# An attention and two mixtures of experts on one core: scores of packed rows in 64x32 tiles, w_in kept as two parts, raw weights in w_out's room

## The chip, the cores and the metric

The kernel runs on one NeuronCore of a Trainium2 chip. The core has a matrix engine (TensorE, PE in the profile, with PEld for its weight loads), VectorE (DVE), ScalarE (ACT), GpSimd (POOL) and SyncE (SP), which only issues transfers here. Each engine works through its own list in order and waits on semaphores. Work memory is SBUF (128 partitions); TensorE writes to PSUM, from where the other engines copy. The metric is the device time of one launch in microseconds; lower is better.

## The reference

```python
def sm_attn(qq, kk, vv):                     # q, k, v: (8, 8, 576, 64); p: (8, 8, 32, 64)
    s = scale * np.matmul(qq, kk.transpose(0, 1, 3, 2))
    s = s - np.max(s, axis=-1, keepdims=True)
    a = np.exp(s)
    a = a / (np.sum(a, axis=-1, keepdims=True) + 1e-09)
    return np.matmul(a, vv)
p_packed = sm_attn(p, k, v)                  # 32 packed rows per head
x = heads side by side of sm_attn(q, p_packed, p_packed)     # (4608, 512)
g = np.maximum(x @ w_in, 0.0) ** 2           # w_in (512, 2048), float64
x = (g @ w_out).astype(np.float32)           # w_out (2048, 512), float64
logits = x @ w_gate + log1p(exp(x @ w_noise)) * noise        # 8 experts
two best experts per token, softmax of their logits as weights
out[token] += weight * (np.maximum(x @ w1[e], 0.0) @ w2[e])  # 512 -> 1024 -> 512
```

The weights w_in and w_out are float64; everything else is float32.

## The kernel before

The work falls into stages. **Packed rows.** For each of 8 batches and two groups of four heads (`part1`, units "A"), 32 packed rows per head attend to 576 keys: scores (`u_s`), maximum, exponent, transposition, product with the values, and a transposition into `pk`, the packed rows with the head dimension on partitions. **Decode.** w_in and w_out come as 64-bit words in 32 chunks of 128 rows by 512 (`decode`, units "d", loads "r"). From the two 32-bit words of a number, ScalarE (`o0`) and VectorE (`o2` to `o5`) make a float32 high part `dec_a` and a bfloat16 rest `dec_b`. For w_in, TensorE adds the two (`o6`) and ScalarE copies the float32 sum into `win` (`o8`). For w_out, a rounded high part and a low part go into `wo`. Raw words lie in four buffers `st`. **Fold.** For each batch and quarter of w_in (`prepare`, units "P"), eight tiles of 64x32 on TensorE multiply packed rows with w_in, so that the second attention and the first layer become one product (`heads`); the result goes as high and low part into `ring`. **Second attention** (`part2`, units "Q"): for each of 16 blocks of 288 tokens, scores of queries with packed rows, softmax, and the attention weights turned into `xT`. **First mixture** (`moe_step`, units "M"): for each block, 16 steps of a first layer (6 matmuls), square, split into `gh` and `gl`, and a second layer (12 matmuls) into four PSUM banks `acc`. At a block's end ScalarE and VectorE copy `acc` to `x2T` (`moe_x2`), VectorE turns it into `x2s` (`x2_turn`, units "X"), and SyncE stores it; logits and routing follow ("R", "U"). **Experts**: tokens are gathered by GpSimd's indirect transfers, and for each of 8 experts in three tiles of rows (512, 384, and 256 with 64 more for four experts) `e_l1` and `e_l2` run two layers; `e_out` weights the rows, and GpSimd adds them to the output.

All precise products are sums of three float32r matmuls over high and low parts (`TERMS`). The order of the first 15 blocks is made by a planner (`schedule`): each unit has an engine, a cost in ns, predecessors and a priority (its longest path to the end and a lead by kind, `AHEAD`); while TensorE would be idle for over 500 ns in the first 45 us of the plan, groups of four matmuls of ones (L1119) are put into its list. Block 15 and the experts are in an order that is written out by hand, in steps that lag two behind each other.

Of the kernel before, what the change touches and what calls it, by code (L numbers as in the profile page):

```python
# [45 lines left out]
STB = 4  # L46
NFF = FF // P
LAG = 2
TB = 3
# [8 lines left out]
AHEAD = {"r": 74, "d": 54.7, "D": 17.3, "a": 113.6, "A": 57.6, "q": 30.5, "Q": 4.5, "p": 73.7, "P": 5.9, "R": 96.4, "M": 1.2, "s": 26.5, "S": 31.5}  # L58
DUE = 11
# [27 lines left out]
def program(ctx, tc, qT, kT, v, v5, pT, w_in, w_out, wg, wn, noise, w1, w2, out):  # L87
# [24 lines left out]
    wo = cst.tile([P, NFF, 2, DM], FR, name="wo")  # L112
# [57 lines left out]
    win = wi.tile([P, 4, FF], F, name="win")  # L170
    att, c_att = open_pool("att", "left")
# [29 lines left out]
    def decode(n):  # L201
# [1126 lines left out]
```

## Time and profile before

| | us |
|---|---|
| median of 3 runs | 1711.03 |
| lowest, highest | 1709.98, 1712.17 |
| the profiled execution | 1707.94 |
| its span, first to last instruction | 1706.1 |
| TensorE busy | 1653.8 |
| VectorE busy | 858.8 |
| ScalarE busy | 638.3 |
| GpSimd busy | 539.4 |

The profiled execution is one run; 1.84 us of its time lie outside the span. A busy time is the union of an engine's instructions; for TensorE the ends are modelled and neighbours overlap, so the price of a piece of its work is better read from the starts.

### The profile page before, as it was taken

The numbers are of one execution on the slowest core, as the hardware profiler recorded it, in microseconds if no ns is written. First come the engines' busy times: TensorE is split into PE (matmuls) and PEld (weight loads), VectorE is DVE, ScalarE is ACT, GpSimd is POOL, SyncE is SP. The second block draws the span as 40 slices with busy tenths as digits, with TensorE's granted clock in tenths as the row PEclk, the third lists the DMA queues.
The fourth block names the chain that finished last, engine by engine and source line by source line (L and its number), as shares of the span: only waits on it lengthen the run. The fifth ranks groups of instructions, "written<-read, shape, count | busy, mean of one in ns | idle before, by whom it ended". The sixth has DMA issues, their size and how long they took to land. (4 is left out here: it accounts for less than half of the span.)

```text
span 1706.1 us, 28402 instructions
## 1 busy us (share of the span) xinstructions
PE 1653.8 (97%) x11054; PEld 1428.1 (84%) x11054; DVE 858.8 (50%) x2008; ACT 638.3 (37%) x1372; POOL 539.4 (32%) x500
## 2 busy tenths in 40 slices
PE   9999999999999999997997999999999999999996
PEld 7678989889898998996786788888888878888785
DVE  6973757565666847474543543333343343434321
ACT  4875444453534445345422222222222232223211
POOL 0000110203020212115326446445364462635611
PEclk9999999999999999999998999999999999999998
DMA  8743142313223202013334434334353443425312
GB/s 258 216 124 87 29 125 54 92 48 91 75 69 97 75 19 59 15 28 91 69 60 102 94 77 102 75 82 98 64 110 71 83 106 63 110 67 103 59 25 32
DMA packets 125343, 140.79 MB, mean 83 GB/s; under 512 B 33055, under 2 KB 87327, under 8 KB 125207
## 3 DMA queue, kind: packets, MB, share of 16 engines
q1 hardware_dynamic: 101975, 100.05, 21.0%
q0 software_dynamic: 23232, 38.90, 13.3%
q8 instruction: 88, 1.44, 0.4%
q14 instruction: 48, 0.39, 0.1%
HBM read 99.71 MB, written 39.19 MB: 81 GB/s over the span
## 5 line engine op out<-in xcount | busy, mean ns | idle before, releaser
L688 PE MATMUL acc<-gh,wo 128*128 128x288 f32 x2048 | 426.5, 301 | 6.6 <-issue 6.6
L688 PEld LDWEIGHTS acc<-gh,wo 128*128 128x128 f32 x2048 | 328.6, 189 | 36.8 <-issue 28.8
L876 DVE SCALAR_TENSOR_TENSOR hl<-ph,hh 128x512 fp32r<-128x512 f32 (+3 forms) x184 | 105.6, 574 | 450.0 <-ACT hh L875 354.4
L843 POOL DMA_INDIRECT xg<-x2d,gi x296 | 295.1, 997 | 90.3 <-issue 87.8
L688 PE MATMUL acc<-gl,wo 128*128 128x288 f32 x1024 | 303.0, 296 | 6.2 <-DVE gl L679 3.1
L875 ACT ACTIVATE hh<-ph 128x512 fp32r<-128x512 f32 (+3 forms) x184 | 92.9, 505 | 504.1 <-PE ph L869 367.2
L652 PE MATMUL ph<-xT,ring 128*128 128x288 f32 x1536 | 245.3, 300 | 4.6 <-issue 3.2
L620 POOL DMA_INDIRECT lst<-ent,pi x96 | 92.6, 965 | 475.3 <-DVE pi L599 238.8
L652 PEld LDWEIGHTS ph<-xT,ring 128*128 128x128 f32 x1536 | 214.8, 189 | 27.2 <-issue 14.6
L869 PE MATMUL ph<-ring,wo 128*128 128x512 f32 (+3 forms) x1152 | 225.8, 344 | 10.4 <-issue 9.3
L898 POOL DMA_INDIRECT out<-y,ls x76 | 125.4, 1650 | 348.9 <-DVE y L895 174.4
L869 PE MATMUL ph<-ring,wb 128*128 128x512 f32 (+3 forms) x1152 | 224.7, 343 | 3.6 <-ACT ring L105 1.9
L869 PEld LDWEIGHTS ph<-ring,wo 128*128 128x128 f32 x1152 | 196.4, 190 | 35.0 <-issue 11.0
L869 PEld LDWEIGHTS ph<-ring,wb 128*128 128x128 f32 x1152 | 194.3, 188 | 29.0 <-ACT ring L105 2.8
L688 PEld LDWEIGHTS acc<-gl,wo 128*128 128x128 f32 x1024 | 193.5, 189 | 9.1 <-DVE gl L679 5.1
L659 ACT ACTIVATE g<-ph 128x288 f32<-128x288 f32 x256 | 104.4, 408 | 242.7 <-PE ph L652 228.7
L886 PE MATMUL acc<-wo,hh 128*128 128x512 f32 (+1 forms) x608 | 193.3, 399 | 0.0
L886 PE MATMUL acc<-wb,hh 128*128 128x512 f32 (+1 forms) x576 | 179.6, 393 | 0.3 <-issue 0.3
L674 DVE TENSOR_TENSOR g<-g 128x288 f32<-128x288 f32 x208 | 101.8, 490 | 116.8 <-ACT gh L665 113.4
L679 DVE TENSOR_TENSOR gl<-g,gh 128x288 fp32r<-128x288 f32 x256 | 117.4, 459 | 54.6 <-ACT gh L105 38.5
L886 PEld LDWEIGHTS acc<-wo,hh 128*128 128x128 f32 (+1 forms) x608 | 111.7, 187 | 23.2 <-issue 0.7
L886 PEld LDWEIGHTS acc<-wb,hh 128*128 128x128 f32 (+1 forms) x576 | 104.8, 185 | 21.4 <-issue 0.8
(202 smaller groups left out, 1763.0 us busy)
## 6 DMA issues: line engine op xcount, KB each, us to landing
wst<-w SPq DMA_DIRECT2D x128, 256.0 KB
out<-zero SPq DMA_DIRECT2D x37, 256.0 KB
q<-qT SPq DMA_DIRECT2D x16, 576.0 KB
x2d<-x2s SPq DMA_DIRECT2D x64, 144.0 KB
kq<-kT SPq DMA_DIRECT2D x15, 576.0 KB
st<-w_in SPq DMA_DIRECT2D x16, 512.0 KB
st<-w_out SPq DMA_DIRECT2D x16, 512.0 KB
vq<-v SPq DMA_DIRECT2D x15, 512.0 KB
```

The source lines that it names most:

```text
L620: nc.gpsimd.indirect_dma_start(out=lst, out_offset=bass.IndirectOffsetOnAxis(ap=st["pi"][:, r, k:k + 1], axis=0), in_=st["ent"][:, r, k], ...
L652: nc.tensor.matmul(ph, w[:, a, d], xT[j, b][:, d], start=n == 0, stop=n == 5)
L659: nc.scalar.activation(g, ph, AF.Relu)
L674: nc.vector.tensor_mul(g, g, g)
L679: nc.vector.tensor_sub(gl, g, gh.bitcast(F))
L688: nc.tensor.matmul(acc[j][d], wo[:, f, b, d * P:(d + 1) * P], g[a], start=f == 0 and n == 0, stop=f == NFF - 1 and n == 2)
L843: nc.gpsimd.indirect_dma_start(out=g[:, x], out_offset=None, in_=src, in_offset=bass.IndirectOffsetOnAxis(ap=idx, axis=0))
L869: nc.tensor.matmul(ph, wblock(e, f, a)[:, c], xt[t][b][:, c, :n], start=i == 0, stop=i == 11)
L875: nc.scalar.activation(hh, ph, AF.Relu)
L876: nc.vector.scalar_tensor_tensor(hl, ph, 0.0, hh.bitcast(F), op0=OP.max, op1=OP.subtract)
L886: nc.tensor.matmul(acc["e", t, r], h[a][:, o:o + n], wblock(e, 8 + f, b).rearrange("p c f -> p (c f)"), start=first and i == 0, stop=last ...
L898: nc.gpsimd.indirect_dma_start(out=out, out_offset=bass.IndirectOffsetOnAxis(ap=sl[:, 0:1], axis=0), in_=y, in_offset=None, compute_op=OP.add)
```

## The change

The scores of packed rows were four matmuls over 128 rows of the array, with packed rows padded with zeros and two columns of tiles. Now they are eight matmuls in tiles of 64x32, one for each of four heads and half of the keys; the host lays out keys and packed rows accordingly. w_in is no longer summed: its high part lies in `win` (float32), its rest in `wint` (bfloat16), and the fold multiplies packed rows with the one and a bfloat16 copy of them, `pk16`, with the other. Raw words are loaded into the room that w_out's finished chunks will take (`wo` is now 16 tiles), which leaves more loads in flight. The second attention's two buffers become one tile of two halves, and `x2s` of the first 14 blocks shares it. In the experts, the extra 64 rows keep high and low part side by side in `pair`, so that one matmul with 128 columns of weights does for two, and `e_out` adds two halves. The planner's leads, costs and due times change.

```diff
-AHEAD = {"r": 74, "d": 54.7, "D": 17.3, "a": 113.6, "A": 57.6, "q": 30.5, "Q": 4.5, "p": 73.7, "P": 5.9, "R": 96.4, "M": 1.2, "s": 26.5, "S": 31.5}
-DUE = 11
+AHEAD = {'r': 77.6, 'o': 80.4, 'd': 83.1, 'D': 20.1, 'a': 85.1, 'A': 60.8, 'q': 35.6, 'Q': 1.1, 'p': 60.4, 'P': 5.9, 'R': 96.4, 'M': 0.9, 's': 34.6, 'S': 32.0}
+DUE = 0
...
-    wo = cst.tile([P, NFF, 2, DM], FR, name="wo")
+    wo = [None] * NFF
+
+    def wo_room(i, shape, dt):
+        return cst.tile(shape, dt, name=f"wo{i}", bufs=1)
...
     win = wi.tile([P, 4, FF], F, name="win")
+    wint = wi.tile([P, 4, FF], BF, name="wint")
...
-        raw[n] = stg.tile([P, 512, 2], I32, name="st", bufs=STB)
+        raw[n] = wo_room(i if kind else 8 + i % 8, [P, 2 * DM], I32)
...
         def o2():
-            st["a"] = stg.tile([P, 512], I32, name="dec_a", bufs=TB)
+            if kind:
+                st["a"] = four(stg.tile([P, 512], I32, name="dec_a", bufs=TB))
+            else:
+                st["a"] = win[:, :, P * i:P * i + P].bitcast(I32)
             nc.vector.tensor_scalar(st["a"], st["t"], 3, 0x7FFFFFFF, op0=OP.logical_shift_left, op1=OP.bitwise_and)
...
         def o5():
-            st["b"] = stg.tile([P, 512], BF, name="dec_b", bufs=2)
-            nc.vector.scalar_tensor_tensor(st["b"], raw[n][:, :, 0].bitcast(U32), 2.0 ** -52, st["t"].bitcast(F),
+            st["b"] = four(stg.tile([P, 512], BF, name="dec_b", bufs=2)) if kind else wint[:, :, P * i:P * i + P]
+            nc.vector.scalar_tensor_tensor(st["b"], words(n, 0).bitcast(U32), 2.0 ** -52, st["t"].bitcast(F),
                                            op0=OP.mult, op1=OP.mult)
...
         def o6():
             st["s"] = side("sum", [P, 512])
-            nc.tensor.matmul(st["s"], ident, st["a"].bitcast(F), start=True, stop=False)
-            if kind:
-                nc.tensor.matmul(st["s"], minus, wo[:, i, 0], start=False, stop=False)
-            nc.tensor.matmul(st["s"], ident16, st["b"], start=False, stop=True)
+            nc.tensor.matmul(st["s"], ident, st["a"].bitcast(F).rearrange("p c f -> p (c f)"), start=True, stop=False)
+            nc.tensor.matmul(st["s"], minus, wo[i][:, 0], start=False, stop=False)
+            nc.tensor.matmul(st["s"], ident16, st["b"].rearrange("p c f -> p (c f)"), start=False, stop=True)
...
         def o7():
-            act_copy(wo[:, i, 0], st["a"].bitcast(F))
+            wo[i] = wo_room(i, [P, 2, DM], FR)
+            act_copy(four(wo[i][:, 0]), st["a"].bitcast(F))
...
         def o8():
-            if kind:
-                act_copy(wo[:, i, 1], st["s"])
-            else:
-                act_copy(win[:, :, P * i:P * i + P], st["s"].rearrange("p (c f) -> p c f", c=4))
+            act_copy(wo[i][:, 1], st["s"])
 
         x = ("d", n)
-        unit(("r", n), "sp", load, [("d", n - STB, 5)], dma=524288)
+        if kind:
+            old = [("d", chunks.index((0, i)), 5)] if i >= 8 else []
+        else:
+            old = [("d", chunks.index((0, i - 8)), 5)] if i >= 8 else []
+        unit(("r", n), "sp", load, old, dma=524288)
...
-        unit(x + (2,), "dve", o2, [x + (0,), ("d", n - TB, 6)], 417)
+        unit(x + (2,), "dve", o2, [x + (0,)] + ([("d", chunks.index((1, i - TB)), 6)] if kind and i >= TB else []) +
+             (lent if not kind and i >= LENT_FROM else []), 417)
...
-        unit(x + (5,), "dve", o5, [x + (4,), ("d", n - 2, 6)], 680)
+        unit(x + (5,), "dve", o5, [x + (4,)] + ([("d", chunks.index((1, i - 2)), 6)] if kind and i >= 2 else []), 680)
         if kind:
-            unit(x + (7,), "act", o7, [x + (3,)], 620)
-        unit(x + (6,), "pe", o6, [x + (5,), x + (7,)] + (lent if not kind and i >= LENT_FROM else []), 1560 if kind else 1300,
-             psum=(x + (8,),))
-        unit(x + (8,), "act", o8, [x + (6,)], 620)
-
-
-    pk = {}
+            unit(x + (7,), "act", o7, [x + (5,)], 620)
+            unit(x + (6,), "pe", o6, [x + (7,)], 1560, psum=(x + (8,),))
+            unit(x + (8,), "act", o8, [x + (6,)], 620)
...
 
         def u_s():
             st["s"] = [side(f"s1{i}", [P, 288]) for i in range(2)]
-            for i in range(2):
-                for c in range(2):
-                    nc.tensor.matmul(st["s"][i][64 * c:64 * c + 64], st["p"][:, c],
-                                     st["k"][:, c, 288 * i:288 * i + 288], start=True, stop=True)
+            for h in range(4):
+                for r in range(2):
+                    o = h % 2
+                    nc.tensor.matmul(st["s"][r][32 * h:32 * h + 32], st["p"][64 * r:64 * r + 64, h // 2, 32 * o:32 * o + 32],
+                                     st["k"][64 * r:64 * r + 64, h // 2, 288 * o:288 * o + 288], start=True, stop=True,
+                                     tile_position=(64 * r, 32 * h))
...
+                pk16[b] = att.tile([P, 2, P], BF, name="pk16", bufs=PKB)
             act_copy(pk[b][:, quad], st["tp"])
+            act_copy(pk16[b][:, quad], st["tp"])
...
-    def heads(b, out, moving):
-        for p in range(4):
-            for r in range(2):
-                k = 64 * p + 32 * r
-                nc.tensor.matmul(out[r][32 * p:32 * p + 32], pk[b].rearrange("p a b -> p (a b)")[64 * r:64 * r + 64, k:k + 32],
-                                 moving[64 * r:64 * r + 64, p], start=True, stop=True, tile_position=(64 * r, 32 * p))
+    def heads(b, out, *terms):
+        for i, (rows, moving) in enumerate(terms):
+            for p in range(4):
+                for r in range(2):
+                    k = 64 * p + 32 * r
+                    nc.tensor.matmul(out[r][32 * p:32 * p + 32], rows[b].rearrange("p a b -> p (a b)")[64 * r:64 * r + 64, k:k + 32],
+                                     moving[64 * r:64 * r + 64, p], start=i == 0, stop=i == len(terms) - 1,
+                                     tile_position=(64 * r, 32 * p))
...
-            heads(b, st["m"], win[:, :, 512 * q:512 * q + 512])
+            heads(b, st["m"], (pk, win[:, :, 512 * q:512 * q + 512]), (pk16, wint[:, :, 512 * q:512 * q + 512]))
...
         unit(x + ("g",), "pe", u_g, [("A", 2 * b, "y"), ("A", 2 * b + 1, "y")] +
-             [("d", chunks.index((0, 4 * q + i)), 8) for i in range(4)] + old, 900, psum=(x + ("l",),) * 2)
+             [("d", chunks.index((0, 4 * q + i)), 5) for i in range(4)] + old, 1140, psum=(x + ("l",),) * 2)
...
-            a = att.tile([P, 2 * BLK], F, name="a2", bufs=1)
+            st["both"] = att.tile([P, 2, 2 * BLK], F, name="a2", bufs=1)
+            a = st["both"][:, 0]
...
-            st["aT"] = att.tile([P, 2, BLK], F, name="aT", bufs=1)
+            st["aT"] = st["both"][:, 1].rearrange("p (d t) -> p d t", d=2)
...
-        unit(x + ("m",), "dve", u_m, [x + ("s",), prev + ("t",)], 2400)
+        unit(x + ("m",), "dve", u_m, [x + ("s",), prev + ("h",), prev + ("d",), ("X", j - 3, "s")], 2400)
...
-        unit(x + ("t",), "dve", u_t, [x + ("n",), prev + ("h",), prev + ("d",)], 680)
+        unit(x + ("t",), "dve", u_t, [x + ("n",)], 680)
...
     def x2_turn(j):
-        x2s[j] = late["p"].tile([P, BLK // 32, 4, 32], F, name="x2s", bufs=1)
+        if j < NS - 1:
+            x2s[j] = att.tile([P, 2, 2 * BLK], F, name="a2", bufs=1).rearrange("p a b -> p (a b)").rearrange("p (g c d) -> p g c d", c=4, d=32)
+        else:
+            x2s[j] = m2["t"].tile([P, BLK // 32, 4, 32], F, name="x2s", bufs=1)
         nc.vector.transpose(x2s[j], x2T[j].rearrange("p c (g t) -> p g c t", t=32))
...
-            unit(y + ("t",), "dve", lambda: x2_turn(j), [("M", j, NFF, d) for d in range(4)] + [("X", j - 1, "s")], 1350)
+            unit(y + ("t",), "dve", lambda: x2_turn(j), [("M", j, NFF, d) for d in range(4)] + [("X", j - 1, "s"), ("Q", j + 2, "h"), ("Q", j + 2, "d")], 1350)
...
-            hh, hl = (m2["a"].tile([P, 4 * P], FR, name=x, bufs=3)[:, :n] for x in ("hh", "hl"))
+            pair, hl = (m2["a"].tile([P, 4 * P], FR, name=x, bufs=3) for x in ("hh", "hl"))
+            hh, hl = pair[:, :n], hl[:, :n]
         nc.scalar.activation(hh, ph, AF.Relu)
-        nc.vector.scalar_tensor_tensor(hl, ph, 0.0, hh.bitcast(F), op0=OP.max, op1=OP.subtract)
-        hs[t, f] = hh, hl
+        full = n - n % P
+        if full < n:
+            nc.vector.scalar_tensor_tensor(pair[:, n:n + EXTRA], ph[:, full:], 0.0, hh[:, full:].bitcast(F), op0=OP.max, op1=OP.subtract)
+        nc.vector.scalar_tensor_tensor(hl[:, :full], ph[:, :full], 0.0, hh[:, :full].bitcast(F), op0=OP.max, op1=OP.subtract)
+        hs[t, f] = hh, hl, pair
...
+        if n == EXTRA:
+            wh, wl = (wblock(e, 8 + f, b).rearrange("p c f -> p (c f)") for b in range(2))
+            for x in (0, 1) if first else (1, 0):
+                nc.tensor.matmul(acc["e", t, r][:n if x else P], h[2][:, o:o + (n if x else P)], wl if x else wh,
+                                 start=first and not x, stop=last and not x)
+            return
...
-        if r % 2:
+        if n == EXTRA:
+            low_part = m2["a"].tile([P, 4, P], F, name="xs", bufs=2).rearrange("p a b -> p (a b)")[:n]
+            act_copy(low_part, acc["e", t, r][n:])
+            nc.vector.tensor_add(y, acc["e", t, r][:n], low_part)
+            nc.vector.tensor_scalar(y, y, sl[:, 1:2].bitcast(F), None, op0=OP.mult)
+        elif r % 2:
```

The planner's result changes nearly everywhere in the first 15 blocks. Three places follow. SyncE's list begins like this before (`kq`, `pq`, `vq` are keys, packed rows and values, `st` the raw words):

```order
L272 DMA kq<-kT 128x1152
L274 DMA pq<-pT 128x128
L272 DMA win<-kT 128x2x576
L274 DMA pq<-pT 128x128
L284 DMA vq<-v 128x1024
L285 DMA vq<-v 64x256
L280 DMA win<-v 128x2x512
L285 DMA win<-v 64x256
L194 DMA st<-w_in 128x1024 x4
L413 DMA q<-qT 128x1152
L272 DMA kq<-kT 128x1152
```

and like this now (`wo_139` and so on are raw words in w_out's room):

```order
L197 DMA wo_139<-w_in 128x1024
L197 DMA wo_141<-w_in 128x1024
L197 DMA wo_143<-w_in 128x1024
L197 DMA wo_145<-w_in 128x1024
L195 DMA wo_147<-w_out 128x1024
L285 DMA kq<-kT 128x1152
L287 DMA pq<-pT 128x128
L197 DMA wo_153<-w_in 128x1024
L195 DMA wo_155<-w_out 128x1024
L285 DMA win<-kT 128x2x576
L287 DMA pq<-pT 128x128
L197 DMA wo_160<-w_in 128x1024
```

Loads of raw words now stand ahead of the first keys, and those of w_out follow early.

On VectorE, at the end of a block of the first mixture (blocks 1 and 2), `x2T` is filled from `acc` and turned into `x2s` before; `gl` is a step's low part and `ring` a fold's:

```order
L395 TENSOR_TENSOR ring<-mp_2362,ring 128x2x256
L395 TENSOR_TENSOR ring<-mp_2363,ring 128x2x256
L695 COPY x2T<-acc_1805 128x288
L674 TENSOR_TENSOR g<-g 128x288
L679 TENSOR_TENSOR gl<-g,gh 128x288
L695 COPY x2T<-acc_1807 128x288
L674 TENSOR_TENSOR g<-g 128x288
L679 TENSOR_TENSOR gl<-g,gh 128x288
L703 STREAM_TRANSPOSE x2s<-x2T 128x1152
```

and now, where `a_2507` is the room shared with the second attention, and the turning is that of the block before:

```order
L461 STREAM_TRANSPOSE a_2362<-a_2362 128x576
L699 TENSOR_TENSOR gl<-g,gh 128x288 x2
L726 STREAM_TRANSPOSE a_2507<-x2T 128x1152
L414 TENSOR_TENSOR ring<-mp_2509,ring 128x2x256
L414 TENSOR_TENSOR ring<-mp_2510,ring 128x2x256
L715 COPY x2T<-acc_1980 128x288
L694 TENSOR_TENSOR g<-g 128x288
L699 TENSOR_TENSOR gl<-g,gh 128x288
L715 COPY x2T<-acc_1982 128x288
```

The turning of a block's result has moved from behind the copies out of `acc` to ahead of the next block's copies.

On TensorE, in the third tile of the first expert (`hh`, `hl` are high and low part of the hidden rows, `wo` the expert's weights), before:

```order
L869 MATMUL ph<-ring,wo 128x320 x12
L886 MATMUL acc_11513<-wo,hh 128x512 x2
L886 MATMUL acc_11513<-wo,hl 128x512
L886 MATMUL acc_11517<-wo,hh 128x512 x2
L886 MATMUL acc_11517<-wo,hl 128x512
L886 MATMUL acc_11521<-wo,hh 64x512 x2
L886 MATMUL acc_11521<-wo,hl 64x512
```

and now:

```order
L892 MATMUL ph<-ring,wo_850 128x320 x12
L920 MATMUL acc_11940<-wo_1489,hh 128x512 x2
L920 MATMUL acc_11940<-wo_1489,hl 128x512
L920 MATMUL acc_11944<-wo_1489,hh 128x512 x2
L920 MATMUL acc_11944<-wo_1489,hl 128x512
L916 MATMUL acc_11948<-wo_1489,hh 64x512
L916 MATMUL acc_11948<-wo_1489,hh 128x512
```

The three matmuls of 64 output rows are now one of 128 and one of 64. Over the whole program, TensorE's list holds 332 matmuls of ones before and 504 now; at its very beginning 52 before and 224 now.

## Rows read from the trace of the kernel before

**Rows 1.** The page: busy share, TensorE's clock by slice, and the code's DMA queue.

```profile
PE 1653.8 (97%) x11054; PEld 1428.1 (84%) x11054; DVE 858.8 (50%) x2008; ACT 638.3 (37%) x1372; POOL 539.4 (32%) x500
...
PEclk9999999999999999999998999999999999999998
...
q8 instruction: 88, 1.44, 0.4%
```

**Rows 2.** Busy time by stretch: us, then each engine's (instructions), clock, DMA share, GB/s.

```profile
30.00:40.00 10.00, 9.01 (x114) 7.17 (x112) 9.59 (x19) 6.65 (x15) 1.41 (x1) 1.00 0.63 229
...
200.00:300.00 100.00, 100.00 (x882) 90.62 (x867) 65.37 (x176) 44.27 (x106) 16.23 (x16) 1.00 0.30 82
...
1000.00:1200.00 200.00, 200.00 (x981) 171.08 (x980) 80.47 (x152) 54.54 (x101) 102.96 (x89) 1.00 0.41 87
```

**Rows 3.** Timeline of TensorE, decode of w_in: start, us, engine, line, operation.

```profile
64.21 1.02 PE L230 MATMUL sum<-dec_a,ident 128*128 128x512 f32 x2
...
65.06 0.38 PE L233 MATMUL sum<-dec_b,ident 128*128 128x512 bf16 x1
```

**Rows 4.** Timeline of TensorE: a bfloat16 term and its successor; a fold and its successor.

```profile
79.55 0.39 PE L233 MATMUL sum<-dec_b,ident 128*128 128x512 bf16 x1
...
79.78 1.02 PE L230 MATMUL sum<-dec_a,ident 128*128 128x512 f32 x2
...
100.92 1.09 PE L374 MATMUL mp<-win,pk 64*32 64x512 f32 x16
...
101.94 0.54 PE L688 MATMUL acc<-gh,wo 128*128 128x288 f32 x2
```

**Rows 5.** Timeline of TensorE: scores of packed rows, scores of queries, each with its successor.

```profile
90.53 1.19 PE L291 MATMUL s<-kq,pq 128*64 128x288 f32 x8
...
91.65 1.07 PE L652 MATMUL ph<-xT,ring 128*128 128x288 f32 x6
...
111.59 0.71 PE L374 MATMUL s<-q,pk 64*32 64x288 f32 x16
...
112.23 1.06 PE L652 MATMUL ph<-xT,ring 128*128 128x288 f32 x6
```

**Rows 6.** Timeline of TensorE: matmuls of ones and what follows them.

```profile
7.91 2.41 PE L1119 MATMUL acc<-ones 128*128 128x128 bf16 x40
...
10.15 0.60 PE L310 MATMUL ta<-ident,a 128*128 128x128 f32 x4
```

**Rows 7.** Timeline of TensorE: the small rows' last matmul in an expert, and its successor.

```profile
950.74 0.40 PE L886 MATMUL acc<-wo,hl 128*64 128x512 f32 x1
...
950.98 2.96 PE L869 MATMUL ph<-ring,wb 128*128 128x512 f32 x12
```

**Rows 8.** Timeline of all engines at the end of block 2.

```profile
209.42 1.68 POOL L449 TENSOR_TENSOR xT<-aT,xT 128x576 fp32r<-128x576 f32 x1 [0.69 <-ACT xT L105]
...
212.48 0.41 ACT L105 ACTIVATE x2T<-acc 128x288 f32<-128x288 f32 x1 [2.37 <-PE acc L688]
...
213.48 1.75 PE L652 MATMUL ph<-xT,ring 128*128 128x288 f32 x12
...
217.48 1.37 DVE L703 STREAM_TRANSPOSE x2s<-x2T 128x1152 f32<-128x1152 f32 x1
```

**Rows 9.** Timeline of VectorE: the last chunk's product.

```profile
110.19 0.69 DVE L225 SCALAR_TENSOR_TENSOR dec_b<-st,dec_t 128x512 bf16<-128x512 uint32 x1
```

**Rows 10.** Timeline of SyncE's queue: first load of keys, first loads of w_in.

```profile
0.75 0.40 SPq L272 DMA_DIRECT2D kq<-kT  x1
...
5.73 3.87 SPq L194 DMA_DIRECT2D st<-w_in  x4
```

**Rows 11.** Busy time by stretch near the end of the last block, columns as above.

```profile
798.00:806.00 8.00, 3.62 (x20) 2.58 (x18) 0.99 (x3) 0.74 (x2) 6.17 (x7) 0.98 0.39 97
...
806.00:816.00 10.00, 4.74 (x18) 4.41 (x19) 2.50 (x10) 2.45 (x5) 2.85 (x4) 0.51 0.26 75
...
816.00:826.00 10.00, 9.04 (x52) 7.26 (x51) 7.84 (x15) 7.39 (x17) 6.62 (x6) 1.00 0.43 91
```

More of the change, by code (lines that the diff above doesn't have):

```diff
@@ L45 @@
 QB, PKB = 1, 2
-STB = 4
 NFF = FF // P
 LAG = 2
-TB = 3
+TB = 2
 WIN = {"pe": 200, "dve": 0, "act": 300, "pool": 900, "sp": 50}
@@ L206, in load, with four @@
             load_raw(n)
+        def four(t):
+            return t.rearrange("p (c f) -> p c f", c=4)
         def o0():
-            st["t"] = stg.tile([P, 512], I32, name="dec_t", bufs=2)
-            nc.scalar.activation(st["t"].bitcast(F), raw[n].bitcast(F)[:, :, 1], AF.Copy, scale=2.0 ** -112)
+            st["t"] = four(stg.tile([P, 512], I32, name="dec_t", bufs=2))
+            nc.scalar.activation(st["t"].bitcast(F), words(n, 1).bitcast(F), AF.Copy, scale=2.0 ** -112)
         def o2():
-            st["a"] = stg.tile([P, 512], I32, name="dec_a", bufs=TB)
+            if kind:
+                st["a"] = four(stg.tile([P, 512], I32, name="dec_a", bufs=TB))
+            else:
+                st["a"] = win[:, :, P * i:P * i + P].bitcast(I32)
             nc.vector.tensor_scalar(st["a"], st["t"], 3, 0x7FFFFFFF, op0=OP.logical_shift_left, op1=OP.bitwise_and)
@@ L612, in u3c @@
                                     rank[:, None, :].to_broadcast([P, E, E]), op=OP.is_equal)
-            pick = late["p"].tile([P, E * E], F, name="t9").rearrange("p (a b) -> p a b", a=E)
+            pick = late["p"].tile([P, E * E], F, name="t9", tag="lT").rearrange("p (a b) -> p a b", a=E)
             nc.vector.tensor_mul(pick, ohe, io8[:, None, :].to_broadcast([P, E, E]))
@@ L687, in moe_l2 @@
             for n, (a, b) in enumerate(TERMS):
-                nc.tensor.matmul(acc[j][d], wo[:, f, b, d * P:(d + 1) * P], g[a],
+                nc.tensor.matmul(acc[j][d], wo[f][:, b, d * P:(d + 1) * P], g[a],
                                  start=f == 0 and n == 0, stop=f == NFF - 1 and n == 2)
@@ L871, in e_l1 @@
         if t == len(tiles) - 1:
-            hh, hl = (wo[:, f, a, :n] for a in range(2))
-        else:
-            hh, hl = (m2["a"].tile([P, 4 * P], FR, name=x, bufs=3)[:, :n] for x in ("hh", "hl"))
+            hh, hl = (wo[f][:, a, :n] for a in range(2))
+            pair = None
+        else:
+            pair, hl = (m2["a"].tile([P, 4 * P], FR, name=x, bufs=3) for x in ("hh", "hl"))
+            hh, hl = pair[:, :n], hl[:, :n]
         nc.scalar.activation(hh, ph, AF.Relu)
-        nc.vector.scalar_tensor_tensor(hl, ph, 0.0, hh.bitcast(F), op0=OP.max, op1=OP.subtract)
-        hs[t, f] = hh, hl
+        full = n - n % P
[3 more added lines that the diff above has]
+        hs[t, f] = hh, hl, pair
     def e_acc(t, f, r, first, last):
@@ L883, in e_acc @@
             bank[0] = (bank[0] + 1) % 6
-            acc["e", t, r] = (ps.tile([P, DM], F, name=f"acc{bank[0]}", bufs=1) if bank[0] < 4 else side("acc4", [P, DM]))[:n]
+            acc["e", t, r] = (ps.tile([P, DM], F, name=f"acc{bank[0]}", bufs=1) if bank[0] < 4 else side("acc4", [P, DM]))[:max(n, 2 * EXTRA)]
+        if n == EXTRA:
[4 more added lines that the diff above has]
+            return
         for i, (a, b) in enumerate(TERMS):
@@ L950, in kind @@
                 return "dD"[chunks[x[1]][0]]
+            if x[0] == "r":
+                return "ro"[chunks[x[1]][0]]
             if x[0] in "XU":
@@ L1181, in program @@
                 c_mo.close()
+                c_mt.close()
                 m2["b"], c_mb = open_pool("m2b", "right")
@@ L1301 @@
     q, k, v, p = i["q"], i["k"], i["v"], i["p"]
-    pT = np.zeros((B, 2, 2, D, 2, 2, NPK), p.dtype)
-    pp = p.reshape(B, 2, 2, 2, NPK, D)
-    for c in range(2):
-        for h in range(2):
-            pT[:, :, h, :, c, h] = pp[:, :, c, h].transpose(0, 1, 3, 2)
+    pT = np.broadcast_to(p.reshape(B, 2, 1, 2, 2, NPK, D).transpose(0, 1, 2, 6, 3, 4, 5), (B, 2, 2, D, 2, 2, NPK))
     v4 = v.reshape(B, 2, 4, S, D).transpose(0, 1, 3, 2, 4).reshape(B, 2, S, 256)
```

18 lines of the change are left out of this document (11 added, 7 removed).

## The prediction

> **What bounds the kernel now.** I read the page first. TensorE is busy for 97% of the span, at the full clock in nearly every slice [rows 1]. So I asked next whether that share is real in each stage, with the busy time by stretch. It is: the engine is busy 9.0 of 10 us while the weights are decoded, 100 of 100 in the steady part and 200 of 200 in the experts [rows 2]. VectorE is nearly as full while the weights are decoded (9.6 of 10 us from 30 to 40 us) and two thirds full later; so VectorE can bound the start, and nothing but TensorE the rest. The reader is to see in these rows that work taken off TensorE is worth its own time, except where TensorE only fills a wait with matmuls of ones, or where VectorE isn't ready. Then I read the timeline of single engines for the price of each piece of TensorE work, as the distance from its start to the start of what follows (a matmul's end is modelled and overlaps the next, so its duration says too much).
>
> **The sums of w_in go.** Each of the 16 chunks of w_in had a float32 and a bfloat16 matmul of 512 columns. The first starts at 64.21 and its partner at 65.06, which is 0.85 us [rows 3]; a bfloat16 matmul of 512 columns holds the engine from 79.55 to 79.78, 0.23 us [rows 4]. That is 1.08 us a chunk, and 16 x 1.08 = 17.3 us less. The 16 copies that ScalarE made of these sums go too; ScalarE bounds nothing here, so I count them at nothing. VectorE writes the same four operations a chunk as before, into the weights' own tile.
>
> **The fold takes a second term.** Each of 32 folds adds 8 bfloat16 matmuls in 64x32 tiles to its 8 float32 ones. Before, a fold holds TensorE from 100.92 to 101.94, 1.02 us for 16 records, two for each tile [rows 4]. The added matmuls make one record for each tile. If the eight tiles run side by side as the eight float32 ones must, the price is that of one bfloat16 matmul of 512 columns, 0.23 us; if a record costs what it does now on average, 8 of 16 records are 0.51 us. I take 0.23, since the row that it is nearest to has the same type and columns and the fold's tiles evidently overlap (eight float32 matmuls of 0.85 us one after the other would be 6.8 us, not 1.02): 32 x 0.23 = 7.4 us more, bound 16.3.
>
> **The scores of packed rows.** Four float32 matmuls of 288 columns in two columns of tiles hold the engine from 90.53 to 91.65, 1.12 us. The new form, eight tiles of 64x32 with 288 columns, already runs in the second attention, from 111.59 to 112.23, 0.64 us [rows 5]. 16 x 0.48 = 7.7 us less. Keys and packed rows keep their bytes, so their loads cost the same.
>
> **The start.** The changed program holds 504 matmuls of ones instead of 332; forty take from 7.91 to 10.15, 0.056 us each [rows 6]. They stand in TensorE's queue whether it would have waited or not: 172 x 0.056 = 9.6 us more. They stand there because the weights' loads are issued ahead of the keys and because less real work is ready in the first 45 us. What this buys is a fuller VectorE at the start; in time I count nothing for it, with bounds of 5 us either way (below).
>
> **The small rows of an expert.** For four experts and eight steps each, three matmuls with 64 rows become two, one of them with high and low part side by side in 128 columns. The one that goes held the engine from 950.74 to 950.98, 0.24 us, in a stage where TensorE has no gaps [rows 7]: 32 x 0.24 = 7.7 us less. VectorE's subtraction splits in two, and four times a copy and an addition follow at a tile's end; VectorE and ScalarE are 40% and 27% full there (80.5 and 54.5 of 200 us) [rows 2], and the bank is not wanted again until six row groups later, so I count these at nothing. Without that cover it would be some 1 us at each of four ends.
>
> **The sum.** -17.3 + 7.4 - 7.7 + 9.6 - 7.7 = -15.7 us. The profiled execution took 1707.94 us, 1706.1 of span and 1.84 around it; with the change 1692.2. The median of the runs stands 3.1 us above the profiled one, so I forecast 1711.0 - 15.7 = 1695 us.
>
> **Waits that are added.** The turned block x2s shares its room with the second attention's scores, so turning block j-1 now waits until block j+1's queries are split by GpSimd, and the copies that empty the accumulators for block j wait for the turning. The room for it at a boundary: GpSimd ends at 209.42 + 1.68 = 211.10, the first copy starts at 212.48, so 1.38 us are free; the turning takes 1.37 us [rows 8]. It just fits, with nothing to spare, on an engine that has other work to do. I take zero for it; the bound is 1.37 us at each of 14 boundaries, 19.2 us. Behind the turning on VectorE stand the next steps' subtractions, for which TensorE waits. The decode's matmuls now wait for ScalarE's copy of the high part where they waited for VectorE; there TensorE has other steps to run.
>
> **The rivals.** First, **VectorE holds the start.** The last chunk's product starts at 110.19 [rows 9], and block 0 can't finish without it. Its work is the same, so it can end earlier only by starting earlier: the first load of w_in is issued at 5.73, and now stands where the keys' load stands, at 0.75 [rows 10], so 5.0 us. My terms give the start 17.3 less, four scores (1.9) less, four folds (0.9) and the ones (9.6) more, 8.7 us; capped at 5.0 the forecast becomes 1695.3 + 3.7 = 1699 us. For it speaks the full VectorE, against it that VectorE also waited in the first 15 us for things that no longer come first.
>
> Second, **the added fold record costs its average share**: 1695.3 + 8.9 = 1704 us. Against it stands the overlap in the 1.02 us.
>
> Third, on the other side, **the shared room chains every boundary.** If the copies wait for the whole turning at all 14 boundaries, 19.2 us come back and the time is 1711.0 - 15.7 + 19.2 = 1714.5 us. It decides against the change from 0.88 us a boundary (15.7 less 3.4, over 14) for no measurable gain, and from 1.36 us on for slower by 0.2%. For it speaks that nothing is to spare at the boundaries where the queries end 2.4 us before the next block (the first matmul of the next block is at 213.48); against it that every other boundary has more room, and that TensorE has the first two steps of the next block to run.
>
> Fourth, **the stalls in the last block move.** From 798 to 816 us TensorE starts 38 matmuls where from 816 to 826 it starts 52 in 10 us: 18 us at that rate would hold 94, so 56 are missing, 10.8 us, part of it at the clock of 1.2 GHz (granted 0.51) after the engine stood [rows 11]. TensorE's code arrives in 88 packets (1.44 MB) for 22,108 records, 251 each (11,054 matmuls and as many weight loads) [rows 1]. The change adds 508 matmuls ahead of the last block by the order (172 of ones, 128 of scores' records, 256 of the fold's, less 48 of the sums), each with its weight load: 1016 records, four packets and a few records. So packets break at nearly the same places of the last block, and I take the stalls as they are. If one goes, 1684 us; if one as large is added, 1706 us.
> The Trainium skill ("Runtime: NRT & Kernel Launch", Instruction fetch mechanics) says that code comes in 16 KiB blocks of 256 instructions and that crossing a block is mostly hidden. The size agrees with the 251 records a packet here. By that rule code would have no part in these stalls, which would then stay; no row says what else TensorE waits for.
>
> **How the numbers follow.** Chances: the sum as it stands, 1688 to 1698, 0.48; VectorE holds the start, 1698 to 1700, 0.14; the dearer fold or smaller waits at boundaries, 1700 to 1706, 0.14; a stall goes, below 1688, 0.12; a stall is added or half the chain, 1706 to 1714, 0.07; the full chain, 0.05. The range runs from 1683 (one stall gone, and a bit) to 1706 (the dearer fold, or one stall more). About 0.2%, 3.4 us, is what a measurement of this kernel can tell from no change: faster needs 1707.6 or less. Faster 0.89, within 0.05, slower 0.06.
>
> **What would show it.** In the changed profile: no sum line for w_in, and 1.1 us less TensorE time for each; a fold at 1.25 us start to start (1.5 would be the second rival); scores at 0.64; 504 matmuls of ones; the first matmul of block 1 some 9 us earlier (5 if VectorE holds); from there to the last block the same time within 2 us, where the third rival would show TensorE waiting at boundaries for copies out of acc; four experts shorter by 1.9 us each; and the stall near the end of the last block, as long as now. The prediction is wrong if block boundaries grow, or if the stalls there do.

## The result and the profile after

The changed kernel takes 1692.7 us (median of 6 runs, 1689.6 to 1698.7) where the kernel before took 1710.1 on the same chip: a ratio of 0.9906 of the means, 95% interval 0.9885 to 0.9928, some 16 us less. The forecast was 1695. The profiled execution took 1693.1 us, 1691.3 of it span; before, 1706.1 of span, so the profiles differ by 14.8 us.

The page of the changed kernel, beside [rows 1]:

```profile
PE 1639.0 (97%) x11524; PEld 1430.2 (85%) x11530; DVE 868.7 (51%) x2044; ACT 635.0 (38%) x1376; POOL 534.7 (32%) x500
...
PEclk9999999999999999998998999999999999999999
...
q8 instruction: 91, 1.49, 0.4%
```

Busy time by stretch, columns as in [rows 2], which the first, fourth and fifth row answer; the last three answer [rows 11]:

```profile
30.00:40.00 10.00, 9.93 (x160) 6.95 (x166) 9.62 (x21) 6.60 (x16) 0.00 (x0) 1.00 1.13 347
40.00:50.00 10.00, 7.97 (x97) 4.30 (x82) 7.91 (x16) 3.89 (x7) 0.00 (x0) 1.00 0.91 265
50.00:60.00 10.00, 7.16 (x45) 6.24 (x46) 9.41 (x19) 5.84 (x14) 1.40 (x1) 0.66 0.69 230
...
200.00:300.00 100.00, 98.73 (x911) 89.71 (x910) 66.40 (x175) 45.73 (x113) 16.29 (x16) 1.00 0.30 80
...
1000.00:1200.00 200.00, 200.00 (x972) 171.55 (x971) 81.71 (x163) 55.73 (x103) 107.43 (x95) 1.00 0.42 91
...
790.00:798.00 8.00, 3.30 (x10) 2.44 (x11) 2.44 (x4) 1.82 (x4) 6.17 (x7) 0.63 0.22 51
798.00:806.00 8.00, 1.88 (x6) 1.71 (x7) 0.69 (x1) 0.87 (x2) 3.83 (x5) 0.50 0.24 58
806.00:816.00 10.00, 9.55 (x58) 8.91 (x57) 7.08 (x21) 6.46 (x15) 5.53 (x6) 0.85 0.44 98
```

The experts are as full as they were, the steady part nearly (98.73 of 100 us). New is a hole from 40 to 60 us (15.1 of 20 us busy, the granted clock at 0.66 in its second half). The kernel before had 19.3 us busy there, at the full clock:

```profile
40.00:50.00 10.00, 9.36 (x40) 5.17 (x39) 9.11 (x21) 9.74 (x24) 0.00 (x0) 1.00 0.80 243
50.00:60.00 10.00, 9.96 (x94) 6.17 (x95) 9.20 (x21) 6.69 (x13) 0.00 (x0) 1.00 0.85 275
```

The stall in the last block is about as long as before, some 7 us earlier.

TensorE's timeline shows the prices: a fold and what follows, a score of packed rows and what follows (beside [rows 4, 5]), the first matmuls of ones (beside [rows 6]), and the small rows of an expert (beside [rows 7]):

```profile
1.06 15.47 PE L1160 MATMUL acc<-ones 128*128 128x128 bf16 x224 [1.06 <-DVE ones L125]
16.47 0.71 PE L305 MATMUL s<-kq,pq 64*32 64x288 f32 x16
...
67.98 1.09 PE L392 MATMUL mp<-win,pk 64*32 64x512 f32 x16
68.87 0.42 PE L392 MATMUL mp<-wint,pk 64*32 64x512 bf16 x8
69.22 0.53 PE L708 MATMUL acc<-gh,wo 128*128 128x288 f32 x2
...
80.37 0.71 PE L305 MATMUL s<-kq,pq 64*32 64x288 f32 x16
81.02 1.06 PE L672 MATMUL ph<-xT,ring 128*128 128x288 f32 x6
...
1247.67 0.62 PE L916 MATMUL acc<-wb,hh 128*128 128x512 f32 x2
1248.14 1.92 PE L892 MATMUL ph<-ring,wb 128*128 128x320 f32 x12
```

A fold holds the engine 1.24 us (1.02 before), a score 0.65, the pair of small rows 0.47 where three matmuls took some 0.70.

Summing over that timeline the distance from each matmul's start to the next one's, by line, gives an account of the time up to block 15's first matmul (762.4 us before, 757.1 now):

| us of TensorE, start to start | before | now | difference | forecast |
|---|---|---|---|---|
| sums (w_in and w_out) | 38.3 | 21.0 | -17.3 | -17.3 |
| matmuls of ones | 23.4 | 31.6 | +8.3 | +9.6 |
| folds | 32.7 | 39.5 | +6.8 | +7.4 |
| scores of packed rows | 19.4 | 15.4 | -4.0 | -7.7 |
| all other lines together | 647.7 | 648.6 | +0.9 | 0 |
| **to block 15** | 761.4 | 756.1 | **-5.3** | **-8.0** |

From there to the first expert it is 61.8 before and 62.1 now (+0.3), and the experts to the end of the span 881.9 and 872.1 (-9.8, forecast -7.7).

The 16 scores fall short by a single wait. The engines around it:

```profile
47.60 0.58 ACT L104 ACTIVATE wo<-sum 128x512 fp32r<-128x512 f32 x1
...
48.23 0.67 PE L305 MATMUL s<-kq,pq 64*32 64x288 f32 x2 [0.23 <-ACT wo L104]
...
51.06 0.69 ACT L104 ACTIVATE xT<-a 128x576 fp32r<-128x576 f32 x1 [2.88 <-DVE a L461]
51.83 1.40 POOL L469 TENSOR_TENSOR xT<-a,xT 128x576 fp32r<-128x576 f32 x1 [49.70 <-ACT xT L104]
52.20 0.58 ACT L104 ACTIVATE wo<-sum 128x512 fp32r<-128x512 f32 x1
52.84 1.21 PE L305 MATMUL s<-kq,pq 64*32 64x288 f32 x14 [3.94 <-ACT wo L104]
53.98 4.51 PE L672 MATMUL ph<-xT,ring 128*128 128x288 f32 x18
...
58.33 0.43 PE L708 MATMUL acc<-gh,wo 128*128 128x288 f32 x2
```

The second tile of the third scores takes a PSUM bank that holds a sum of w_out. ScalarE's copy of it (52.20) stands behind the copy of block 0's attention weights (51.06), which waits for VectorE; so TensorE stands for 3.9 us. And block 0 couldn't have gone on sooner: its `xT` is complete at 51.83 + 1.40 = 53.2, and the first layer starts at 53.98. The 18 matmuls behind the hole take 4.35 us, 0.24 each, at the low level of the clock (1.2 GHz; the granted clock is 0.50 from 54 to 58 us).

### The profile page after: what moved, and what is told of

Its sections match the earlier page's. It is cut to its first block, busy times and chain, and to the rows that moved or that the text cites. A ratio compares the mean times of both kernels' runs of the same rounds, so it can differ in the third digit from the quotient of the medians.

```text
span 1691.3 us, 29415 instructions
## 1 busy us (share of the span) xinstructions
PE 1639.0 (97%) x11524; PEld 1430.2 (85%) x11530; DVE 868.7 (51%) x2044; ACT 635.0 (38%) x1376; POOL 534.7 (32%) x500
## 5 line engine op out<-in xcount | busy, mean ns | idle before, releaser
L904 DVE SCALAR_TENSOR_TENSOR hl<-ph,hh 128x512 fp32r<-128x512 f32 (+2 forms) x184 | 103.2, 561 | 377.8 <-ACT hh L900 303.1
L892 PE MATMUL ph<-ring,wo 128*128 128x512 f32 (+3 forms) x1152 | 227.2, 345 | 11.4 <-issue 10.0
L920 PE MATMUL acc<-wo,hh 128*128 128x512 f32 x576 | 182.8, 399 | 0.0
L920 PE MATMUL acc<-wb,hh 128*128 128x512 f32 x544 | 169.2, 392 | 0.9 <-DVE y L934 0.9
L694 DVE TENSOR_TENSOR g<-g 128x288 f32<-128x288 f32 x208 | 105.3, 506 | 112.3 <-ACT gh L685 110.9
L920 PEld LDWEIGHTS acc<-wo,hh 128*128 128x128 f32 x576 | 107.1, 190 | 21.0 <-issue 0.5
L920 PEld LDWEIGHTS acc<-wb,hh 128*128 128x128 f32 x544 | 100.4, 188 | 19.8 <-DVE y L934 1.4
```

Of the source, the lines that this page charges most:

```text
L694: nc.vector.tensor_mul(g, g, g)
L892: nc.tensor.matmul(ph, wblock(e, f, a)[:, c], xt[t][b][:, c, :n], start=i == 0, stop=i == 11)
L904: nc.vector.scalar_tensor_tensor(hl[:, :full], ph[:, :full], 0.0, hh[:, :full].bitcast(F), op0=OP.max, op1=OP.subtract)
L920: nc.tensor.matmul(acc["e", t, r], h[a][:, o:o + n], wblock(e, 8 + f, b).rearrange("p c f -> p (c f)"), start=first and i == 0, stop=last ...
```

## The experiments

The first four ran on a chip where the kernel before takes 1677.0 us, the others on chips where it takes 1710.4 to 1710.6, as it did for the result. So the stages are compared by the start of a stage's first matmul in the profiled executions (us):

| run | block 0 | block 1 | block 15 | first expert | end |
|---|---|---|---|---|---|
| before | 36.7 | 121.4 | 762.4 | 824.2 | 1706.1 |
| changed | 54.0 | 113.7 | 757.1 | 819.2 | 1691.3 |
| e1 small rows as before | 52.3 | 111.8 | 757.1 | 807.0 | 1672.6 |
| e2 scores as before | 54.2 | 114.4 | 764.0 | 813.2 | 1670.0 |
| e3 172 fewer ones | 51.0 | 110.3 | 756.2 | 808.0 | 1667.7 |
| e4 80 ones in the hole | 52.7 | 112.4 | 755.0 | 804.3 | 1662.5 |
| e5 the changed kernel again | 53.3 | 112.7 | 756.5 | 820.8 | 1692.3 |
| e6 no ones | 49.0 | 108.3 | 753.6 | 818.2 | 1690.4 |
| e7 less on VectorE | 53.0 | 112.5 | 754.2 | 817.8 | 1693.4 |
| e8 sums back | 61.7 | 130.4 | 774.1 | 837.4 | 1709.2 |
| e9 sums back, no ones | 57.9 | 126.4 | 768.9 | 849.8 | 1719.4 |
| e10 turning twice | 53.0 | 112.3 | 757.9 | 823.0 | 1697.0 |
| e11 old order | 52.9 | 119.0 | 760.0 | 815.7 | 1690.4 |
| e12 no ones but 80 | 51.3 | 110.0 | 754.6 | 817.6 | 1693.0 |

Up to the experts the changed kernel, e1 and e5 are the same program: block 1 starts at 113.7, 111.8 and 112.7 there, block 15 at 757.1, 757.1 and 756.5. From block 1 to block 15 all but the kernel before, e2, e10 and e11 have the same work in the same order, and take 641.7 to 645.9 us for it. So 2 us at block 1 can be scatter, and so can some 2 us either way that show first at block 15. The profiled execution of e9 (1721.2 us) is one of its longest, by the last block; its start is used here.

**e1, the small rows undone.**

```diff
-        if n == EXTRA:
-            wh, wl = (wblock(e, 8 + f, b).rearrange("p c f -> p (c f)") for b in range(2))
...
-            return
         for i, (a, b) in enumerate(TERMS):
```

> The changed kernel with the small rows of an expert multiplied as before, in three matmuls of 64 rows. Theory (TensorE's work in the experts is worth its own time): one matmul of 0.23 us comes back in 32 places, 7.3 us, so 1692.7 + 7.3 = 1700 us, and the trace shows 1.8 us more for each of four experts. Rival (the gain of 9.8 us in the experts came from elsewhere, from shorter stalls in the first expert): the time stays within 3 us of 1692.7.

1672.4 us, 0.9973 (0.9963 to 0.9984) of the kernel before there. From the first expert to the end it takes 865.6 us, the other three of that chip 856.8, 859.7 and 858.2, on average 858.2: +7.4 us. The term holds. The other 2.4 of the 9.8 us seen at first are not told from scatter: with the changed experts that stretch takes 869.6 to 875.6 us in the nine kernels on the other chips.

**e2, the scores undone.**

```diff
-            for h in range(4):
-                for r in range(2):
...
+            for i in range(2):
+                for c in range(2):
+                    nc.tensor.matmul(st["s"][i][64 * c:64 * c + 64], st["p"][:, c],
+                                     st["k"][:, c, 288 * i:288 * i + 288], start=True, stop=True)
```

> The changed kernel with the scores of packed rows as before, four matmuls over 128 rows, and the host's old layout of keys and packed rows; everything else and the order are the changed kernel's. Theory (each of 16 scores is worth its difference, 1.21 - 0.65 = 0.56 us): 9 us more in all if none is hidden; the first three lie among matmuls of ones or waits, so 13 x 0.56 = 7.3 us more, 1700 us. Rival (VectorE holds the first 110 us, and eleven of the sixteen scores lie there): only the scores after that cost, five at most, 2.8 us, 1695.5 us.

1673.6 us, ratio 0.9982 (0.9973 to 0.9991). Block 15 starts at 764.0, 6.9 to 7.5 us later than in the changed kernel. In the account by line the scores take 6.9 us more than in e1, 5.6 of them behind block 1's start. The rival's count was wrong: only four of the sixteen scores lie before block 1 now.

**e3, 172 ones fewer.**

```diff
         if x == ("warm",):
+            groups_of_ones += 1
+            if groups_of_ones <= 43:
+                continue
```

> The changed kernel without the first 172 of the 224 matmuls of ones that TensorE's list begins with. Theory of the prediction (the ones are work like any other): 172 x 0.056 = 9.6 us less, 1683 us. Rival (TensorE would only wait there, for keys that land later): the first scores start where they do now, at 16.5 us, give or take 1 us, and the time stays within 2 us of 1692.7; if the granted clock then falls to half in the first 30 us, up to 3 us more. Also: the change of 344 records ahead of the last block is 1.4 packets of code, so if code sets the stall at 792 to 806 us, it moves by some 90 records, about 45 matmuls or two and a half steps; if it belongs to the work there, it stays at the same step.

1669.5 us, 0.9954 (0.994 to 0.9968). The first scores start at 11.4 us, not at 15 to 16.5: the ones did hold them, but the gain shrinks to 2.4 us at block 1 (against e5; 1.5 against e1 on the same chip) and to 0.3 to 0.9 at block 15, which scatter can explain. The theory's 9.6 us and the rival's standstill at 16.5 both fall. The long stall of the last block is missing in all four kernels on this chip, so this run can't say whether code sets its place; the short waits there stay behind the same instructions (the `rk` matmuls, the last step ahead of the third tile).

**e4, ones in the hole.**

```diff
+            if x == ("A", 2, "s"):
+                for k in range(80):
+                    nc.tensor.matmul(hot[:, :P], ones, ones, start=True, stop=True)
```

> The changed kernel with 80 more matmuls of ones ahead of the third scores, where TensorE stands from 48.9 to 52.8 us and the granted clock falls to half from 51.3 to 58.2. Theory (the wait there is for the attention of block 0, and its cost goes on in the slow clock): the ones take 80 x 0.056 = 4.5 us from time that was idle, the clock stays at 2.4 GHz and the 18 first-layer matmuls behind take 2.4 instead of 4.35 us, so 2 us less, 1690.7 us. Rival (VectorE holds the start whatever the clock): no change, 1692.7. If the ones stand in the way, up to 1 us more.

1664.5 us, 0.9929 (0.9915 to 0.9943). TensorE's timeline there:

```profile
47.00 4.63 PE L1164 MATMUL acc<-ones 128*128 128x128 bf16 x80
51.56 1.18 PE L305 MATMUL s<-kq,pq 64*32 64x288 f32 x16
52.67 2.65 PE L672 MATMUL ph<-xT,ring 128*128 128x288 f32 x18
55.19 0.53 PE L708 MATMUL acc<-gh,wo 128*128 128x288 f32 x2
57.16 0.40 PE L708 MATMUL acc<-gl,wo 128*128 128x288 f32 x1 [1.44 <-DVE gl L699]
```

The 18 matmuls take 2.52 us where they took 4.35 (3.75 in e1, on the same chip), and the granted clock is 1.00 from 50 to 60 us: so far the theory holds. But the gain goes no further. Behind them TensorE waits 1.44 us for `gl`, which VectorE, 9.90 of 10 us busy from 50 to 60 us, comes to no sooner. From the first matmul of block 0 to the first with `gl` it takes 4.49 us, against 4.24 in e1, 4.26 in e5 and 4.62 in the changed kernel, and block 1 starts at 112.4, amid the 111.8 to 113.7 of the unfilled kernel. Block 15's start, 1.5 to 2.1 us earlier, is within the scatter of the stretch between. So here the rival's "no change" is what the trace supports.

**e5, control.**

> The changed kernel itself, on the chip of the other three, since the kernel before took 1677 us on the chip of the first four and 1710 us on the one before. All theories expect the 0.9906 of the first comparison, if chips differ only in a part that both kernels have; if the shorter time of the last block and the first expert on that chip is worth less to the changed kernel, a ratio nearer to 1.

1694.8 us against 1710.6: 0.9900 (0.9883 to 0.9916), the first result again. It ran on another chip than the one it was meant for, so the ratio on the faster chip stays unmeasured.

**e6, no ones.**

```diff
-            for k in range(4):
-                nc.tensor.matmul(hot[:, :P], ones, ones, start=True, stop=True)
+            pass
```

> The changed kernel without any of its 504 matmuls of ones. Theory (they only fill TensorE's waits; the start is held by the loads, then by VectorE): block 1 starts within 3 us of where it does with them, the time within 4 us either way, and the granted clock falls to half in stretches of the first 50 us. The prediction's term (ones are work like any other, 0.056 us each): 504 x 0.056 = 28 us less, or at least the 9.6 us of the 172 that were added.

1696.5 us, 0.9917 (0.99 to 0.9933). Block 1 starts 4.4 us earlier than in e5, block 15 2.9: a seventh of the 31.6 us that the ones fill. The time is no shorter than in e5 (1694.8). What the ones fill is seen in TensorE's waits of the first 60 us without them (total, times, longest):

```profile
PE s L305 <- DMA pq<-pT: 11.8, 1, 11.8
PE s L305 <- ACT wo L104: 4.2, 2, 3.9
PE ta L325 <- ACT a L319: 2.3, 1, 2.3
PE sum L242 <- ACT a L319: 1.9, 1, 1.9
PE mp L392 <- DVE ring L414: 1.8, 1, 1.8
```

**e7, less on VectorE.**

```diff
         def o4():
-            nc.vector.tensor_scalar(st["t"], st["a"], -0x00800000, None, op0=OP.bitwise_and)
+            pass
```

> The changed kernel without the third of VectorE's four operations on each of the 32 chunks (the mask of the exponent is left out, 0.42 us each, 13.4 us in all; the low words are then weighted wrongly). Theory (VectorE holds the start): block 1 starts earlier, by up to 25 x 0.42 = 10 us where VectorE is full all the time, and by at least 4 us; the time follows. Rival (TensorE's sum sets the start, as the prediction had it): TensorE's list is as long as before, so block 1 starts within 1.5 us of where it does now.

1695.1 us, 0.991 (0.9897 to 0.9923). VectorE's busy time from 10 to 50 us falls from 33.6 (e5) to 29.0, and block 1 starts 0.2 us earlier. Block 15 starts 2.3 us earlier, within the scatter behind block 1. With the ones in the list VectorE doesn't hold the start. (Without the ones this wasn't tried.)

**e8 and e9, the sums put back**, with the ones and without.

```diff
+            if x[0] == "P" and x[1] == 0 and x[3] == "g":
+                s = side("sum", [P, 512])
+                for i in range(4 * x[2], 4 * x[2] + 4):
+                    nc.tensor.matmul(s, ident, win[:, :, P * i:P * i + P], start=True, stop=False)
+                    nc.tensor.matmul(s, ident16, wint[:, :, P * i:P * i + P], start=False, stop=True)
             units[x][3]()
```

> The changed kernel with the 16 sums of w_in put back on TensorE, a float32 and a bfloat16 matmul of 512 columns for each chunk, four ahead of each fold of block 0; nothing reads the result, and ScalarE's copies stay away. The prediction's term: 16 x 1.08 = 17.3 us more, less what the wait of 4 us at 49 us hides, so 13 to 17 us more. Rival (VectorE holds the start, and the removed sums only made room that matmuls of ones now fill): block 1 starts later by less than 9 us.

1710.4 us, ratio 1.000 (0.9987 to 1.0013). Block 1 starts 17.7 us later than in e5: the sums alone undo the change's whole gain.

> The 16 sums put back as in the run before, and none of the 504 matmuls of ones; nothing reads the sums. Against the run without ones, where block 1 started at 108.3 us: theory (TensorE's waits, which the ones fill, come before the folds of block 0, and a fold's sums can't start before its chunks are there): most of the sums' 17.3 us stands behind the waits, so block 1 starts 12 to 17 us later, at 120 to 125 us. Rival (the waits would have hidden the sums): less than 8 us later, before 116 us.

1706.2 us, 0.9986 (0.9962 to 1.0011). Block 1 starts 18.1 us later than in e6. So the waits that the ones fill would not have hidden the sums: they come before the decoded chunks are there, the sums after. That is shown for sums right ahead of the folds; the places among the decode that the planner gave them before were not tried.

**e10, the turning twice.**

```diff
-        nc.vector.transpose(x2s[j], x2T[j].rearrange("p c (g t) -> p g c t", t=32))
+        for _ in range(2 if j < NS - 1 else 1):
+            nc.vector.transpose(x2s[j], x2T[j].rearrange("p c (g t) -> p g c t", t=32))
```

> The changed kernel with the turning of a block into the shared room done twice at each of the first 14 boundaries, 1.37 us more on VectorE each time (ScalarE's copies out of acc wait for the second). The third rival of the prediction (the room chains the boundaries): 14 x 1.37 = 19.2 us more. Theory (ScalarE waits for the turning, 13.7 us in six places now, but TensorE has steps of the next block to run): at most one in three boundaries shows it, 0 to 6 us more at the start of block 15, 1693 to 1699 us.

1696.5 us, 0.9916 (0.9892 to 0.9941). ScalarE waits for the turning 24.2 us in 11 places, but block 15 starts 0.8 to 1.4 us later, of 19.2 added, and even that can be scatter.

**e11, the old leads.**

```diff
-DUE = 0
+AHEAD = {"r": 74, "o": 74, "d": 54.7, "D": 17.3, "a": 113.6, "A": 57.6, "q": 30.5, "Q": 4.5, "p": 73.7, "P": 5.9, "R": 96.4, "M": 1.2, "s": 26.5, "S": 31.5}
+DUE = 11
```

> The changed kernel with the planner's leads and due times of before (loads of w_out with the lead of the others). Theory (the sum of TensorE's work makes the time, the order only places it): the time stays within 5 us of 1692.7, with another count of ones at the start. Rival (the new order is what lets the start end earlier): block 1 starts 5 us or more later.

1697.9 us, 0.9929 (0.9901 to 0.9956). It too has 512 ones, with its first scores at 6.0 us, so the count of ones doesn't come from the loads' place. Block 1 starts 6.3 us later than in e5, but block 15 only 3.5: the order gives some 3 us at most, not the gain.

**e12, no ones but 80.** The edits of e6 and e4 together.

> The changed kernel without its 504 matmuls of ones but with 80 ahead of the third scores: the two edits that gained, together. Theory (the early ones delay the first scores by 3 to 4 us, and the 80 keep the clock at 2.4 GHz through the wait for block 0's attention): both gains add up, block 1 at 107 us instead of 112.7, 4 to 6 us less at block 15, 1687 to 1689 us on a chip where the changed kernel takes 1693 to 1695. Rival (either gain is given back before block 15): within 2 us of the changed kernel.

1694.7 us, 0.9896 (0.987 to 0.9922), not told apart from e5. Block 1 starts 2.7 us earlier, block 15 1.9, less than without the 80 ones (e6), so the gains don't add. Block 0 starts 2.3 us later than in e6 (51.3 against 49.0), but 1.7 of that is there at its scores, ahead of the 80 (39.92 against 38.20 us). The 80 end at 50.7, and `xT` is complete at 48.60 + 1.40 = 50.0: they stand in the way by less than 1 us.

## Why the prediction was right, step by step

- **The sums of w_in go, -17.3.** -17.3 in the account; +17.7 and +18.1 at block 1 when put back. Right in size and place.
- **The fold's second term, +7.4.** +6.8, 0.21 a fold. The second rival (0.51) falls.
- **The scores, -7.7.** 0.65 as forecast; e2 gives 6.9 to 7.5 back. Right. In the account only -4.0 shows, since the new wait stands in that line.
- **The ones, +9.6.** Right in the account (+8.3) and wrong as a cause. The prediction called them work that stands there whether TensorE would have waited or not; e6 shows that all 504 cost 4.4 us at block 1, and nothing that the runs tell from zero in the whole time. They measure the waits: taking the sums away left TensorE with less to do while keys land and the first chunks are decoded. It was luck that the term is a fair price for waits that are there in any case.
- **Waits counted at nothing.** This step failed: 3.9 us at 49 to 53, and then the low clock. The prediction looked at the waits of the shared room and not at what the new order puts in ScalarE's queue ahead of a bank's copy. In the account it stands for 3.7 us, more than the 2.7 missing at block 15 (ones and folds took less than forecast, the other lines 0.9 more). What it costs in the end is not shown: no run takes it away, block 0's attention holds the next step until 53.2 anyway, and in e4, which fills it, the gain of the faster clock is lost in a wait for VectorE.
- **The start.** Block 1's first matmul came 7.7 us earlier (9 forecast, 5 by the first rival). The first rival, VectorE, falls with e7, e8 and e9: its last product of a chunk, forecast to end earlier or hold block 0, starts at 113.0 us against 110.19 [rows 9], and block 1 is earlier all the same. Only where TensorE gets ahead, as in e4, does it wait for VectorE's `gl`.
- **The shared room, 0.** The third rival's wait is there, but on ScalarE: 13.7 us in six places. TensorE has the next block's steps to run, and e10 shows that even the double costs some 1 us, if anything. What TensorE does wait for at boundaries is 4.6 us in five places (2.9 in three before), and it is another cause, shown at the end.
- **The small rows, -7.7.** 7.4 by e1. Right.
- **The stalls in the last block.** As long as before: +0.3. But the fourth rival's frame, code packets that break at certain places, isn't borne out. Counted in TensorE's timeline, the long stall (distances that stay over 0.68 us) begins 220 and 231 matmuls behind block 15's first in the two executions of the changed kernel, and 225 behind it in e8, where 48 more matmuls lie ahead. It is missing in all four kernels on the chip of e1, and in e11 it begins at 190, so the work alone doesn't set it either. The Trainium skill ("Runtime: NRT & Kernel Launch", Instruction fetch mechanics) has crossings of a code block mostly hidden; nothing here speaks against it.
- **The sum.** -14.8 measured by the profiles, -15.7 forecast, by two misses that nearly cancel: the start gave 2.7 less, the experts 2.1 more. Those 2.1 lie within the scatter of that stretch (869.6 to 875.6 us with the same experts); so the closeness of the sum is in part luck. The fold's added matmuls and the raw words' new room were not undone by themselves. On the chip of e1 the changed kernel itself wasn't run; e1's time less its 7.4 us is 1665, an estimate, 0.7% under the kernel before there.

## What to carry to other kernels

Work that comes after the last wait of a stage is worth its whole time on the bound engine, even where the stage as a whole is full of waits; put it back once with the fillers and once without to see that. Filler on the bound engine is no cost to be summed: take all of it out and look how far the next stage moves. Filler that keeps the clock up is worth something only if no other engine takes the gain: look at the next wait. When an order changes, ask of each PSUM bank which copy frees it, and what that copy stands behind in its engine's queue.

## What the hardware showed that was not expected

**VectorE stands while GpSimd subtracts.** At the end of block 2 in the changed kernel, beside [rows 8]:

```profile
207.14 2.10 DVE L694 TENSOR_TENSOR g<-g 128x288 f32<-128x288 f32 x1 [1.36 <-ACT gh L685]
...
207.49 1.42 POOL L469 TENSOR_TENSOR xT<-a,xT 128x576 fp32r<-128x576 f32 x1
...
209.34 0.46 DVE L699 TENSOR_TENSOR gl<-g,gh 128x288 fp32r<-128x288 f32 x1
209.71 1.37 DVE L726 STREAM_TRANSPOSE a<-x2T 128x1152 f32<-128x1152 f32 x1
209.85 0.41 PE L708 MATMUL acc<-gl,wo 128*128 128x288 f32 x1 [1.27 <-DVE gl L699]
...
211.18 0.41 ACT L104 ACTIVATE x2T<-acc 128x288 f32<-128x288 f32 x1 [2.18 <-DVE a L726]
...
211.29 1.76 PE L672 MATMUL ph<-xT,ring 128*128 128x288 f32 x12
```

A square of 0.46 us takes 2.10 around GpSimd's 1.42, the low part behind it is late, and TensorE waits 1.27 us; ScalarE's wait of 2.18 us for the turning holds nobody, the next block starts at 211.29. The Trainium skill ("SBUF — State Buffer", Who interferes with whom) says that a VectorE instruction with two SBUF inputs contends with a GpSimd instruction that reads SBUF; the trace agrees. It is so in the kernel before too (2.25 us at its boundary at 302 us).

**The clock in the rows and the pace of matmuls.** In e6 the granted clock reads 1.00 from 10 to 30 us, yet a pair of sum matmuls is shown with 2.07 us at 20.37, right after a wait, and with 1.02 at 28.13.

**A trickle that depends on the chip.** From 793 to 806 us in the changed kernel, and within two steps of there in every kernel on the chips where the one before takes 1710 us, TensorE's matmuls mostly start 0.7, 1.4, 2.1 or 2.8 us apart, with no releaser, while ScalarE and VectorE stand too (0.87 and 0.69 us busy of 8, above). On the chip where it takes 1677 us, e4 has in the same stretches:

```profile
790.00:798.00 8.00, 5.78 (x39) 4.97 (x37) 4.84 (x17) 3.16 (x7) 6.15 (x7) 1.00 0.50 148
798.00:806.00 8.00, 7.80 (x43) 6.20 (x44) 6.07 (x11) 6.49 (x15) 6.13 (x6) 1.00 0.51 115
```

The last block takes 49 to 52 us there; on the others 62 to 65, but 55.7 in e11 and 80.9 in e9, so the trickle also differs from run to run. No run here shows the cause.
